# Polysketch attention and hash routing on one core: the first heads taken one by one, and routing steps reordered

## The chip, the core and the metric

The kernel runs on one core of a Trainium2 chip. The metric is the device time of one launch in microseconds (us); lower is better. A core has five engines that run side by side, each with a queue of its own, in order: TensorE (PE) multiplies matrices, VectorE (DVE), ScalarE (ACT) and GpSimd (POOL) work element by element, and SyncE (SP) here only issues transfers. PE's weight loads stand in the profile as PEld. Transfers (DMA) are issued from SP and ACT, gathers and scatters by lists of rows from POOL.

## What is computed

Attention without a softmax: q and k are mapped to 64 features, the products of two sketches of 8 numbers each, and k's features are summed with v into one 64 x 32 matrix per head. Its output, as 4352 rows of 128, goes to a mixture of experts in which a token's number alone picks one of 8 experts.

```python
def phi(x):                                   # q, k, v: (4, 4, 1088, 32)
    a = np.einsum('rd,bhsd->bhsr', S1, x)     # S1, S2: (8, 32)
    b = np.einsum('rd,bhsd->bhsr', S2, x)
    return np.einsum('bhsi,bhsj->bhsij', a, b).reshape(*x.shape[:-1], r * r)
q_p, k_p = (phi(q), phi(k))
kv = np.einsum('bhsf,bhsd->bhfd', k_p, v)
z = np.sum(k_p, axis=2)
num = np.einsum('bhsf,bhfd->bhsd', q_p, kv)
den = np.einsum('bhsf,bhf->bhs', q_p, z)[..., None] + 1e-06
attn = num / den
x = attn.transpose(0, 2, 1, 3).reshape(4352, 128)
expert_idx = token_ids * np.int64(2654435761) % np.int64(8)
# for each expert e, rows of its tokens:
out[mask] = np.maximum(x[mask] @ w1[e], 0.0) @ w2[e]      # w1: (8, 128, 1024), w2: (8, 1024, 128)
```

## The kernel before

Every engine's order is written by hand: `tc.manual_schedule` (L92) keeps instructions on each engine in the order of the program's text. What sets the order around the change is therefore the order of calls, and each engine waits where an operand isn't there yet.

Attention goes over 4 batches, b = 0 to 3, each with 4 heads (H) of 1088 rows: 1024 in the main part, 8 rows (T) to each of 128 partitions, and 64 in a tail; the tails of all batches are worked together in batch 0. The steps of a batch, with the tiles' names:

- `load_main` (L114) loads k, q and v of a batch by SP; only k of batch 0 comes in two parts of two heads. `load_tail` loads the tails. Loads of later batches are held back by a one-element write on ACT (`A.memzero`) into the tile.
- `turned`, `turned_all` (L472, L483): PE transposes 4 rows of a head at once (T_ps), 8 transposes per tensor, in two banks of PSUM; ACT copies them to kT or qT. The pool of these banks (`bank`) has 4.
- `s_products` (L505): PE multiplies kT or qT by S (ab_ps); both sketches come out. S itself is given as 64-bit numbers: DVE turns them into 32 bits (s_rep), and PE and DVE spread them (`s_turned`, L282).
- `first_copied` (ACT) copies the first sketch, `features` (DVE, L527) multiplies it by the second: kp for k, f for q, two instructions each.
- `values` (POOL, a part by ACT in batch 0) copies v into va, with a column of ones beside it; `kv_products` (PE, L554) sums kp times va into kv, `kv_diagonal` (ACT) copies kv to m.
- `q_turned` (L581): PE transposes f (fT_ps), ACT and DVE copy it to fT by the list EVICT = (A, V, A, V); `x_products` multiply fT by m into xe.
- `denominators` (DVE), `x_main` and `x_tail` (POOL) divide: xs; `x_rows` (SP) stores them to a table in DRAM, x_rows.

Routing is spread between these steps, mostly on DVE: `route_scan` numbers the tokens of each expert, `route_counts` sums over partitions on PE, `route_places` and `route_order` rank the experts by load, `route_bases` and `route_ranks` give every token a digit, `route_parts` and `route_slots` (with a chain on POOL) its slot, `route_in_tile`, `route_rows` and `route_tiles` make one-hot matrices, and `route_list` multiplies them on PE into the list of rows (get, put). The name pos is used for the place of a token and, after its last use in `route_slots`, for another value, which the loop for overflow at the end reads.

Then come the experts: 16 groups of about 256 to 320 tokens. POOL gathers their rows by the list from x_rows (`fetch_tile`), PE transposes the first groups' rows (`bring`; later groups are transposed by DMA), `layer1` and `layer2` multiply, and POOL scatters the results. The gathers of the first group (of batches 0 and 1 alone) wait for the stores of both batches. `beside` (L1006) lists what stands between the products: `at(g, c, f)` puts f after step c of group g; `bring(1)` stands at step 6 of group 0, and layer1 of group 1 follows step 7.

Before all this PE runs six products of no use (`keep_busy(WARM)`, L219), on tiles of ones.

Of the kernel before, what the change touches and what calls it, by code (L numbers as in the profile page):

```python
# [30 lines left out]
def kernel(  # L31
# [64 lines left out]
    for i, (s, eng) in enumerate(((S1, nc.sync), (S2, nc.scalar))):  # L96
        eng.dma_start(s64[i * R:(i + 1) * R], _words(s).rearrange("r (d two) -> r d two", two=2))
# [16 lines left out]
    def load_main(src, b, tag, ahead=None):  # L114
        t = load.tile([P, H, T, D], F32, tag=tag, name=f"{tag}{b}")
        if ahead:
            ahead(t[:, 0, 0, 0:1])
        rows = src[b, :, 0:SM, :].rearrange("h (p t) d -> p h t d", t=T)
        parts = 2 if (b, tag) == (0, "k") else 1
        for i in range(parts):  # L120
            hs = slice(i * H // parts, (i + 1) * H // parts)
            nc.sync.dma_start(t[:, hs], rows[:, hs])
        return t
# [46 lines left out]
    k_tail = load_tail(k, "k_tail")  # L170
    k_t.append(load_main(k, 1, "k"))
    q_t.append(load_main(q, 1, "q"))
    q_tail = load_tail(q, "q_tail")
    v_tail = load_tail(v, "v_tail")
    k_t.append(load_main(k, 2, "k"))
# [43 lines left out]
    def keep_busy(n):  # L219

        if n == 0:
            return
        p = ps_o.tile([P, 512], F32, tag="o", name="idle")
        for _ in range(n):
            nc.tensor.matmul(p[:], warm[:].to_broadcast([P, P]), warm[:].to_broadcast([P, 512]), start=True, stop=True)
# [153 lines left out]
    late, slot, gap, over = (const.tile([P, C], F32, name=n) for n in ("late", "slot", "gap", "over"))  # L379
# [9 lines left out]
    def route_slots():  # L389

        V_ = nc.vector
        V_.tensor_scalar(late[:], pos[:], 0.0, 1.0, op0=OP.max, op1=OP.min)
# [7 lines left out]
        V_.scalar_tensor_tensor(pos[:], place_t[:], float(GD), pos[:], op0=OP.mult, op1=OP.add)  # L400

        G_ = nc.gpsimd
        G_.tensor_scalar(over[:], pos[:], float(GL), 0.0, op0=OP.subtract, op1=OP.max)
# [146 lines left out]
    def values(b, ts=slice(0, T), copy=nc.gpsimd.tensor_copy):  # L550

        copy(vas[b % 2][:, ts, :, 0:D], v_t[b][:, :, ts].rearrange("p h t d -> p t h d"))  # L552

    def kv_products(b, kp, ts, kv=None):  # L554

        kv = kv or x_bank([P, H // 2, DA], "kv")
        for t in ts:
            (f, v_) = (kp[:, t], vas[b % 2][:, t]) if t < T else (f_tail[:, 0, b % TT], va_tails[b // TT][:, b % TT])
            for pr in range(H // 2):
                for h in range(2):  # L560
                    nc.tensor.matmul(kv[h * R * R:(h + 1) * R * R, pr], f[:, 2 * pr + h].rearrange("p i j -> p (i j)"),  # L561
                                     v_[:, 2 * pr + h], start=(t == 0 and pr == 0), stop=(t == T), skip_group_check=True,
                                     tile_position=(0, h * R * R))
        return kv
# [157 lines left out]

    def turn_in(k):
# [12 lines left out]

    A, V = nc.scalar, nc.vector
    EVICT = (A, V, A, V)
    s_turned(x_bank)
    kT, half = turned(k_t[0], "kT")  # L740
    for pr in range(H // 2):
        for g in range(GQ):
            hs = slice(2 * pr, 2 * pr + 2)
            nc.scalar.copy(kT[:, g, hs], half(g, range(H)[hs])[:])
    route_experts()
    route_scan()
    nc.scalar.copy(cp[:], seq[:, :, C - 1])
# [6 lines left out]
    values(0, slice(0, T // 2))  # L754
    qT = turned_all(q_t[0], "qT")
    cnt = route_counts()
    route_places(cnt)
    route_order()
    abq, aq, f = ab_bank(), first_of_ab(), feature_tile("f")
    s_products(abq, qT, range(GQ))  # L760
    first_copied(aq, abq, range(GQ))
    values(0, slice(T // 2, T), nc.scalar.copy)
    kv = kv_products(0, kp, range(T))
    features(f, aq, abq, range(GQ))
    kT = turned_all(k_t[1], "kT")
    route_bases(cnt)
    digits = route_ranks()
    route_order_end()
# [10 lines left out]
    for b in range(B - 1):  # L779
        last = b == B - 2  # L780
        if b > 0:
# [5 lines left out]
        fT = q_turned(f, (A, A, A, A) if last else EVICT)  # L787
        if b == 0:
            tail_ps = bank([P, 2, TT, P], "tail_ps")
# [5 lines left out]
            for u, va_tail in enumerate(va_tails):  # L795
                rows = tail_rows(u * TT)
                nc.gpsimd.tensor_copy(va_tail[rows, :, :, 0:D], v_tail[rows])
            route_parts(digits)
            tail_features(tail_products(tailT))
# [21 lines left out]
        if b == 0:  # L821
            q_t.append(load_main(q, 2, "q", A.memzero))
            kv_products(0, None, range(T, T + 1), kv)
            m = kv_diagonal(0, kv)
            tail_f_turned()
        values(b + 1)
        if b == 1:
            v_t.append(load_main(v, 3, "v", A.memzero))
            for g in range(GQ):
                x_rows(0, g)  # L830
            x_tail_rows(0)
            route_rows(0)
            route_tiles()
            route_rows(1)
# [7 lines left out]
        if last:  # L842
            load_expert(0, (2,), A.memzero)
            features(kp, ak, abk, range(GQ))
# [4 lines left out]
        if not last:  # L849
            for g in range(GQ):  # L850
                x_main(b, g, nc.gpsimd)
            x_tail(b, nc.gpsimd)
# [169 lines left out]
    at(0, 6, bring, 1, o_bank)  # L1022
# [96 lines left out]
    with tc.If(turns > 0):  # L1119
        with tc.For_i(0, turns):  # L1120
# [20 lines left out]
            nc.vector.tensor_scalar(at[:], pos[:], of[:, 1:2], float(GL), op0=OP.subtract, op1=OP.subtract)  # L1141
# [69 lines left out]
```

## Time and profile before

| | us |
|---|---|
| median of 3 runs | 178.16 |
| lowest, highest | 177.83, 178.74 |
| the profiled execution | 180.07 |
| its span, first to last instruction | 178.1 |
| PE busy in the span | 171.0 |
| DVE busy | 98.0 |
| POOL busy | 94.6 |
| ACT busy | 66.9 |

A profile shows one execution, whose own time is 180.07 us; the span is what lies between its first and last instruction. Durations come from it, so a sum of them is to be compared with 180.07, not with the median. Times in the text count from the span's start. A timeline row has start, duration, engine, line, operation, the tiles out<-in with their shapes, the number of instructions merged, and in brackets the idle time before it with what ended it. A line can be that of a helper that several steps share. The list of waits has, for each pair, the total, the count and the longest; these are its largest rows that are not in the experts' part:

```profile
POOL va L552 <- DMA v<-in_v_dram: 6.5, 2, 3.8
POOL over L403 <- DVE pos L400: 5.0, 1, 5.0
ACT m L570 <- PE kv L561: 4.8, 3, 2.3
ACT first_of_ab L525 <- PE ab_ps L510: 3.7, 6, 0.7
```

### The profile page before, as it was taken

What the parts mean: (1) busy time and instruction counts of PE and PEld (TensorE: products, weight loads), DVE (VectorE), ACT (ScalarE), POOL (GpSimd) and SP (SyncE); (2) the same over time, 40 slices, a digit from 0 to 9 for tenths busy, and PEclk for the clock granted to TensorE, in tenths of its full rate; (3) what the DMA queues carried; (4) which work ended last, traced back from release to release, by engine and by line L of the source; (5) the groups of instructions that cost most, each with busy time, mean ns of one, the idle gap of its engine ahead of it and who ended that gap; (6) DMA issues with size and microseconds to landing.
All of it is one profiled execution on the core that took longest, in us unless ns stands there. A gap on an engine that the chain in (4) does not pass through costs nothing. (4 is left out here: it accounts for less than half of the span.)

```text
span 178.1 us, 4338 instructions
## 1 busy us (share of the span) xinstructions
PE 171.0 (96%) x1569; PEld 144.5 (81%) x1569; DVE 98.0 (55%) x312; ACT 66.9 (38%) x179; POOL 94.6 (53%) x134
## 2 busy tenths in 40 slices
PE   6999999999999999999999999999999999999990
PEld 1899899999987888888777777788888777778990
DVE  5589999996945425365444343634457552442330
ACT  3456685874643242232341323233141332321330
POOL 7324239364176657177776612775655760406752
PEclk9999999999999999999999999999999999999999
DMA  4998057565495969994992663386342522210111
GB/s 131 296 250 241 13 145 250 139 254 172 141 292 166 317 170 189 168 309 103 234 166 75 186 170 74 103 213 142 78 96 53 117 65 54 56 36 29 43 36 32
DMA packets 39302, 25.83 MB, mean 145 GB/s; under 512 B 20884, under 2 KB 35477, under 8 KB 39280
## 3 DMA queue, kind: packets, MB, share of 16 engines
q1 hardware_dynamic: 36880, 20.98, 46.9%
q0 software_dynamic: 2240, 4.53, 9.0%
q8 instruction: 13, 0.21, 0.5%
q14 instruction: 9, 0.07, 0.1%
q10 hardware_dynamic: 160, 0.04, 0.1%
HBM read 17.41 MB, written 4.52 MB: 123 GB/s over the span
## 5 line engine op out<-in xcount | busy, mean ns | idle before, releaser
L897 PE MATMUL op<-hT,w 128*128 128x256 f32 (+8 forms) x256 | 76.3, 389 | 0.0
L650 DVE TENSOR_SCALAR hT<-hp 128x256 f32<-128x256 f32 (+9 forms) x68 | 29.1, 427 | 57.2 <-PE hp L889 54.7
L897 PEld LDWEIGHTS op<-hT,w 128*128 128x128 f32 x256 | 47.5, 190 | 10.5
L900 POOL DMA_INDIRECT out_dram<-os,put x35 | 35.3, 1008 | 28.3 <-DVE os L958 11.8
L648 ACT ACTIVATE hT<-hp 128x256 f32<-128x256 f32 (+9 forms) x68 | 26.6, 391 | 63.0 <-PE hp L889 62.9
L642 POOL DMA_INDIRECT xg<-x_rows,idx x33 | 34.0, 1030 | 28.4 <-DVE idx L709 17.4
L889 PE MATMUL hp<-xT_late,w 128*128 128x320 f32 (+8 forms) x144 | 41.7, 385 | 0.0
L889 PE MATMUL hp<-xT,w 128*128 128x256 f32 x128 | 37.6, 382 | 0.1
L889 PEld LDWEIGHTS hp<-xT_late,w 128*128 128x128 f32 x144 | 25.3, 190 | 4.7
L889 PEld LDWEIGHTS hp<-xT,w 128*128 128x128 f32 x128 | 23.9, 190 | 5.9 <-ACT hT L648 0.5
L532 DVE TENSOR_TENSOR f<-first_of_ab,ab_ps 128x1024 f32<-128x1024 f32 x8 | 9.4, 1212 | 1.8 <-ACT first_of_ab L525 1.8
L958 DVE COPY os<-turned 128x256 uint16<-128x256 uint16 (+1 forms) x26 | 7.7, 336 | 4.1 <-DMA turned<-half 3.9
L532 DVE TENSOR_TENSOR kp<-first_of_ab,ab_ps 128x1024 f32<-128x1024 f32 x8 | 9.3, 1200 | 1.2 <-ACT first_of_ab L525 1.2
L561 PE MATMUL kv<-va,kp 128*64 128x33 f32 x256 | 8.6, 224 | 0.1
L552 POOL COPY va<-v 128x1024 f32<-128x1024 f32 (+1 forms) x4 | 3.7, 932 | 9.2 <-DMA v<-in_v_dram 6.5
L561 PEld LDWEIGHTS kv<-va,kp 128*64 128x64 f32 x256 | 8.0, 138 | 0.8 <-ACT va L552 0.2
L597 PE MATMUL x_ps<-m,fT 128*64 128x66 f32 x256 | 8.3, 222 | 0.0
L597 PEld LDWEIGHTS x_ps<-m,fT 128*64 128x64 f32 x256 | 7.8, 137 | 0.5 <-issue 0.3
L937 ACT COPY half<-op 128x256 uint16<-128x256 uint16 x16 | 5.2, 375 | 7.5 <-PE op L897 7.5
L578 PE MATMUL fT_ps<-ident,f 128*128 128x128 f32 x64 | 7.7, 273 | 0.0
L623 POOL TENSOR_TENSOR xs<-xe,den 128x512 f32<-128x512 f32 x6 | 6.7, 1142 | 1.4 <-ACT qT L486 1.4
L728 DVE COPY xh<-xg 128x256 uint16<-128x256 uint16 (+1 forms) x26 | 6.9, 307 | 0.5 <-DMA xg<-x_rows,idx 0.5
(190 smaller groups left out, 170.5 us busy)
## 6 DMA issues: line engine op xcount, KB each, us to landing
w<-in_moe_w_dram SPq DMA_DIRECT2D x22, 256.0 KB, 4.5
w<-in_moe_w_dram SPq DMA_DIRECT2D x5, 512.0 KB, 4.6
q<-in_q_dram SPq DMA_DIRECT2D x4, 512.0 KB, 4.5
v<-in_v_dram SPq DMA_DIRECT2D x4, 512.0 KB
x_rows<-xs SPq DMA_DIRECT2D x8, 256.0 KB
k<-in_k_dram SPq DMA_DIRECT2D x3, 512.0 KB
out_dram<-os,put POOLq DMA_INDIRECT x35, 2.6
xg<-x_rows,idx POOLq DMA_INDIRECT x33, 3.4
```

Source lines behind the costliest of these rows:

```text
L532: nc.vector.tensor_tensor(dst[:].rearrange("p t h i j -> p (t h) i j")[:, r], a[:, r].unsqueeze(3).to_broadcast(shape), rows_of_ab(ab)[:, ...
L561: nc.tensor.matmul(kv[h * R * R:(h + 1) * R * R, pr], f[:, 2 * pr + h].rearrange("p i j -> p (i j)"), v_[:, 2 * pr + h], start=(t == 0 and ...
L578: nc.tensor.transpose(p[:, t, pr], f[:, 2 * i + t, 2 * pr:2 * pr + 2].rearrange("p h i j -> p (h i j)"), ident[:])
L597: nc.tensor.matmul(p[r, t, 2 * pr:2 * pr + 2].rearrange("p h d -> p (h d)"), fT[:, lo + t, pr, r], m[:, pr].rearrange("p h d -> p (h d)"), ...
L642: nc.gpsimd.indirect_dma_start(out=dst, out_offset=None, in_=x_dram[0:rows], in_offset=bass.IndirectOffsetOnAxis(ap=idx, axis=0), bounds_c ...
L648: nc.scalar.activation(dst, src, AF.Relu if relu else AF.Copy)
L650: return nc.vector.tensor_scalar(dst, src, 0.0, None, op0=OP.max).ins
L728: nc.vector.tensor_copy(xh[:, x * w:(x + 1) * w], _half(xg3[k][:].rearrange("p a b -> p (a b)")[:, 0:w], x))
L889: nc.tensor.matmul(hp[:, 0:hi - lo], w1[:, g % E, c * P:(c + 1) * P], x_columns(first_of(g) + lo, first_of(g) + hi), start=True, stop=True)
L897: nc.tensor.matmul(ops[g][:, 0:hi - lo], w2[:, g % E, c], hTs[g][:, c, lo:hi], start=(c == 0), stop=(c == FC - 1))
L900: st_ = nc.gpsimd.indirect_dma_start(out=out[:], out_offset=bass.IndirectOffsetOnAxis(ap=idx, axis=0), in_=src, in_offset=None, bounds_che ...
L958: nc.vector.tensor_copy(_half(os[:].rearrange("p a b -> p (a b)"), x)[:, 0:n * DM], tts[x][:, 0:n].rearrange("p a b -> p (a b)"))
```

## The change

- Loads: both parts of S are issued from ACT. k and q of batch 0 come in four parts, a head each, v of batch 0 in two. In SP's order k and q of batch 1 go ahead of the tails, k of batch 2 ahead of v's tail.
- First batch: `turned_head` transposes one head of k or q (two transposes, one bank, one copy of 256 columns on ACT). For k, S is spread after the third head. For q, each head's products with S follow the next head's transposes; their bank comes from another pool (`x_bank`). Behind the products of k stand two products of no use (`keep_busy(2, bank)`).
- `values` of batch 0 is split by heads instead of rows, the first half on ACT, the second on POOL; kv goes first over the first pair of heads, then over the second. `route_scan` follows the features of k on DVE, and `route_counts` follows kv on PE; features of q come ahead of `route_places`.
- Batch 0: `route_bases` and `route_ranks` go behind the copies of fT, `tail_features` ahead of `route_parts`, `route_order_end` last. k of batch 2 is transposed in batch 0, half ahead of the tail's kv and half behind fTt_ps. ACT makes all copies of fT in batch 1.
- xs of batch 0: its denominators, divisions and stores go to batch 1, behind the one-hot matrices.
- `route_slots` writes a tile of its own, behind, first, where the last step wrote pos; POOL's chain and the loop for overflow read it.
- `bring(1)` becomes two steps of one tile each, at steps 5 and 6, both copied by DVE.

```diff
--- before
+++ after
@@ -93,8 +93,8 @@
     s64 = const.tile([2 * R, D, 2], I32)
-    for i, (s, eng) in enumerate(((S1, nc.sync), (S2, nc.scalar))):
-        eng.dma_start(s64[i * R:(i + 1) * R], _words(s).rearrange("r (d two) -> r d two", two=2))
+    for i, s in enumerate((S1, S2)):
+        nc.scalar.dma_start(s64[i * R:(i + 1) * R], _words(s).rearrange("r (d two) -> r d two", two=2))
     tok = const.tile([P, C, 2], I32)
@@ -116,7 +116,7 @@
         rows = src[b, :, 0:SM, :].rearrange("h (p t) d -> p h t d", t=T)
-        parts = 2 if (b, tag) == (0, "k") else 1
+        parts = {(0, "k"): H, (0, "q"): H, (0, "v"): H // 2}.get((b, tag), 1)
         for i in range(parts):
@@ -167,12 +167,12 @@
     v_t.append(load_main(v, 0, "v"))
-    k_tail = load_tail(k, "k_tail")
     k_t.append(load_main(k, 1, "k"))
     q_t.append(load_main(q, 1, "q"))
+    k_tail = load_tail(k, "k_tail")
     q_tail = load_tail(q, "q_tail")
+    k_t.append(load_main(k, 2, "k"))
     v_tail = load_tail(v, "v_tail")
-    k_t.append(load_main(k, 2, "k"))
     v_t.append(load_main(v, 1, "v"))
@@ -216,11 +216,11 @@
-    def keep_busy(n):
+    def keep_busy(n, psum=None):
...
...
             return
-        p = ps_o.tile([P, 512], F32, tag="o", name="idle")
+        p = psum([P, 512], "idle") if psum else ps_o.tile([P, 512], F32, tag="o", name="idle")
         for _ in range(n):
@@ -376,7 +376,7 @@
-    late, slot, gap, over = (const.tile([P, C], F32, name=n) for n in ("late", "slot", "gap", "over"))
+    late, slot, gap, over, behind = (const.tile([P, C], F32, name=n) for n in ("late", "slot", "gap", "over", "behind"))
...
@@ -389,6 +389,7 @@
         V_ = nc.vector
+        V_.scalar_tensor_tensor(behind[:], place_t[:], float(GD), pos[:], op0=OP.mult, op1=OP.add)
         V_.tensor_scalar(late[:], pos[:], 0.0, 1.0, op0=OP.max, op1=OP.min)
@@ -397,10 +398,9 @@
         V_.scalar_tensor_tensor(slot[:], place_t[:], float(GE), slot[:], op0=OP.mult, op1=OP.add)
-        V_.scalar_tensor_tensor(pos[:], place_t[:], float(GD), pos[:], op0=OP.mult, op1=OP.add)
...
         G_ = nc.gpsimd
-        G_.tensor_scalar(over[:], pos[:], float(GL), 0.0, op0=OP.subtract, op1=OP.max)
+        G_.tensor_scalar(over[:], behind[:], float(GL), 0.0, op0=OP.subtract, op1=OP.max)
         G_.tensor_scalar(over[:], over[:], float(2 * ST * P), None, op0=OP.mult)
@@ -547,16 +547,16 @@
-    def values(b, ts=slice(0, T), copy=nc.gpsimd.tensor_copy):
-
-        copy(vas[b % 2][:, ts, :, 0:D], v_t[b][:, :, ts].rearrange("p h t d -> p t h d"))
-
-    def kv_products(b, kp, ts, kv=None):
+    def values(b, hs=slice(0, H), copy=nc.gpsimd.tensor_copy):
+
+        copy(vas[b % 2][:, :, hs, 0:D], v_t[b][:, hs].rearrange("p h t d -> p t h d"))
+
+    def kv_products(b, kp, ts, kv=None, pairs=range(H // 2)):
...
...
             (f, v_) = (kp[:, t], vas[b % 2][:, t]) if t < T else (f_tail[:, 0, b % TT], va_tails[b // TT][:, b % TT])
-            for pr in range(H // 2):
+            for pr in pairs:
                 for h in range(2):
@@ -720,6 +720,12 @@
+    def bring_tile(k, j):
+        i = tiles_of(k)[0] + j
+        xp = o_bank([P, P], "xp")
+        nc.tensor.transpose(xp[:], xg3[k][:, j], ident[:])
+        evict(1, x_columns(i * P, (i + 1) * P), xp[:])
+
     def turn_in(k):
@@ -734,38 +740,52 @@
+    def x_main_all(b):
+        for g in range(GQ):
+            x_main(b, g, nc.gpsimd)
+        x_tail(b, nc.gpsimd)
+
     A, V = nc.scalar, nc.vector
     EVICT = (A, V, A, V)
-    s_turned(x_bank)
-    kT, half = turned(k_t[0], "kT")
-    for pr in range(H // 2):
+    kT, _ = turned(k_t[0], "kT")
+
+    def turned_head(src, sT, h):
+        p = bank([P, GQ, P], "T_ps")
         for g in range(GQ):
-            hs = slice(2 * pr, 2 * pr + 2)
-            nc.scalar.copy(kT[:, g, hs], half(g, range(H)[hs])[:])
+            nc.tensor.transpose(p[:, g], src[:, h, g * Q:(g + 1) * Q].rearrange("p t d -> p (t d)"), ident[:])
+        nc.scalar.copy(sT[:, :, h], p[:])
+
+    for h in range(H):
+        turned_head(k_t[0], kT, h)
+        if h == 2:
+            s_turned(x_bank)
     route_experts()
-    route_scan()
-    nc.scalar.copy(cp[:], seq[:, :, C - 1])
     ak, kp = first_of_ab(), feature_tile("kp")
...
         features(kp, ak, abk[g], [g])
-    values(0, slice(0, T // 2))
-    qT = turned_all(q_t[0], "qT")
+    route_scan()
+    keep_busy(2, bank)
+    qT, _ = turned(q_t[0], "qT")
+    abq, aq, f = ab_bank(x_bank), first_of_ab(), feature_tile("f")
+    for h in range(H + 1):
+        if h < H:
+            turned_head(q_t[0], qT, h)
+        if h > 0:
+            s_products(abq, qT, range(GQ), [h - 1])
+    values(0, slice(0, H // 2), nc.scalar.copy)
+    first_copied(aq, abq, range(GQ))
+    values(0, slice(H // 2, H))
+    kv = kv_products(0, kp, range(T), pairs=(0,))
+    kv_products(0, kp, range(T), kv, (1,))
+    nc.scalar.copy(cp[:], seq[:, :, C - 1])
     cnt = route_counts()
+    features(f, aq, abq, range(GQ))
     route_places(cnt)
     route_order()
-    abq, aq, f = ab_bank(), first_of_ab(), feature_tile("f")
-    s_products(abq, qT, range(GQ))
-    first_copied(aq, abq, range(GQ))
-    values(0, slice(T // 2, T), nc.scalar.copy)
-    kv = kv_products(0, kp, range(T))
-    features(f, aq, abq, range(GQ))
     kT = turned_all(k_t[1], "kT")
-    route_bases(cnt)
-    digits = route_ranks()
-    route_order_end()
...
@@ -778,14 +798,16 @@
         last = b == B - 2
-        if b > 0:
+        if b > 1:
             kT = turned_all(k_t[b + 1], "kT")
...
             qT = turned_all(q_t[b + 1], "qT")
-        fT = q_turned(f, (A, A, A, A) if last else EVICT)
+        fT = q_turned(f, (A, A, A, A) if b > 0 else EVICT)
         if b == 0:
+            route_bases(cnt)
+            digits = route_ranks()
             tail_ps = bank([P, 2, TT, P], "tail_ps")
@@ -795,8 +817,9 @@
                 nc.gpsimd.tensor_copy(va_tail[rows, :, :, 0:D], v_tail[rows])
+            tail_features(tail_products(tailT))
             route_parts(digits)
-            tail_features(tail_products(tailT))
+            route_order_end()
         elif not last:
@@ -820,18 +843,23 @@
             q_t.append(load_main(q, 2, "q", A.memzero))
+            kT, half = turned(k_t[2], "kT")
+            nc.scalar.copy(kT[:, 0], half(0)[:])
             kv_products(0, None, range(T, T + 1), kv)
...
             tail_f_turned()
+            nc.scalar.copy(kT[:, 1], half(1)[:])
         values(b + 1)
...
             v_t.append(load_main(v, 3, "v", A.memzero))
+            route_rows(0)
+            route_tiles()
+            route_rows(1)
+            denominators(0)
+            x_main_all(0)
             for g in range(GQ):
...
             x_tail_rows(0)
-            route_rows(0)
-            route_tiles()
-            route_rows(1)
         features(f, aq, abq, range(GQ))
@@ -841,15 +869,16 @@
             load_expert(0, (2,), A.memzero)
+        if b == 0:
+            features(kp, ak, abk, range(GQ))
+        elif last:
             features(kp, ak, abk, range(GQ))
...
             features(kp, ak, abk, range(GQ))
-        if not last:
-            for g in range(GQ):
-                x_main(b, g, nc.gpsimd)
-            x_tail(b, nc.gpsimd)
+        if 0 < b and not last:
+            x_main_all(b)
         if b == 1:
@@ -1019,7 +1048,8 @@
         at(0, 3 + c, fetch_tile, 3, c)
-    at(0, 6, bring, 1, o_bank)
+    for j in range(tiles_of(1)[1]):
+        at(0, 5 + j, bring_tile, 1, j)
     at(1, 5, bring, 2)
@@ -1138,7 +1168,7 @@
             at = moe.tile([P, C], F32, tag="at", name="at", bufs=1)
-            nc.vector.tensor_scalar(at[:], pos[:], of[:, 1:2], float(GL), op0=OP.subtract, op1=OP.subtract)
+            nc.vector.tensor_scalar(at[:], behind[:], of[:, 1:2], float(GL), op0=OP.subtract, op1=OP.subtract)
             nc.vector.tensor_mul(at[:], at[:], own[:])
...
             rows = moe.tile([P, C, P], BF16, tag="hT", name="rows", bufs=2)
...
```

## The prediction

> **What bounds the kernel now.** I read the page first: TensorE (PE) is busy 171.0 us of 178.1, the next engine, VectorE (DVE), 98.0 us. Its slices say where PE is not full:
>
> ```profile
> span 178.1 us, 4338 instructions
> PE   6999999999999999999999999999999999999990
> DVE  5589999996945425365444343634457552442330
> ```
>
> Only the first slice (4.45 us each) and the end are thin. But busy is not full rate: the page says that ends of matmuls are modelled. So I took the timeline of PE and compared equal groups early and late:
>
> ```profile
> 0.98 2.74 PE L225 MATMUL idle<-warm 128*128 128x512 bf16 x6 [0.98 <-POOL warm L180]
> 4.75 0.26 PE L284 MATMUL s_ps<-ident,s_rep 16*128 16x16 f32 x1 [1.03 <-POOL is_early L211]
> 4.93 1.97 PE L477 MATMUL T_ps<-ident,k 128*128 128x128 f32 x8
> 6.83 1.98 PE L510 MATMUL ab_ps<-s_k,kT 128*64 128x64 f32 x32
> 8.74 1.80 PE L477 MATMUL T_ps<-ident,q 128*128 128x128 f32 x8
> ...
> 11.73 2.29 PE L561 MATMUL kv<-va,kp 128*64 128x33 f32 x64
> 13.95 1.09 PE L477 MATMUL T_ps<-ident,k 128*128 128x128 f32 x8
> 14.88 1.91 PE L578 MATMUL fT_ps<-ident,f 128*128 128x128 f32 x16
> ```
>
> Eight transposes take 1.97 us at 4.93 and 1.09 at 13.95; 32 products with S take 1.98 at 6.83 and (later rows) 1.10. PE runs at about half rate until some 10.2 us and then at the full one to the end. From 13.95 on groups follow one another with hardly a hole: between 58 and 170 us, the stretch table gives PE 112.00 of 112.00. So the end is set by when PE reaches L477 for k1 (13.95), plus the few holes after it. These I looked for as irregular gaps: T_ps of q1 takes 1.36 us at 17.06 instead of 1.06 to 1.09, because its bank waits for DVE's copy of fT (L585), which stands behind routing steps; kv of the tail waits at 21.05 for f_tail, ready at 20.91; around `bring(1)` some 0.4 us are lost:
>
> ```profile
> 17.04 1.27 DVE L585 COPY fT<-fT_ps 128x512 f32<-128x512 f32 x2
> 19.70 1.21 DVE L543 TENSOR_TENSOR f_tail<-first_of_ab,abt_ps 128x1024 f32<-128x1024 f32 x1
> ```
>
> Last, POOL, for what may hold PE at 48.07, the first gathered rows:
>
> ```profile
> 28.18 2.61 POOL L623 TENSOR_TENSOR xs<-xe,den 128x512 f32<-128x512 f32 x2
> 30.75 1.44 POOL L629 TENSOR_TENSOR xs_tail<-xe,den 64x128 f32<-64x128 f32 x1
> 34.90 1.05 POOL L552 COPY va<-v 128x1024 f32<-128x1024 f32 x1 [2.70 <-PE T_ps L477]
> 37.35 2.06 POOL L623 TENSOR_TENSOR xs<-xe,den 128x512 f32<-128x512 f32 x2 [1.41 <-ACT qT L486]
> 39.36 0.42 POOL L629 TENSOR_TENSOR xs_tail<-xe,den 64x128 f32<-64x128 f32 x1
> 39.73 1.03 POOL L552 COPY va<-v 128x1024 f32<-128x1024 f32 x1
> 42.77 1.29 POOL L642 DMA_INDIRECT xg<-x_rows,get  x1 [2.01 <-issue]
> ```
>
> The wait at 34.90 is named after PE, but v2's transfer, issued at 28.77, ends at about the same time, and that is what the copy needs.
>
> **What the Trainium skill says.** "TensorE: Matmul & The Clock Gate", section "What's actually happening": PE starts at half clock and gets the full one after a busy window of about 3.4 us; windows run free of the kernel. The trace agrees with half and full (421 against 273 ns for one transpose). Work from 0.98 to 3.7, then a hole of 1.03 us, was not enough here; the step came at about 10.2. The same page, "PE-mode transpose", says that transposes don't count as busy for this; the window that ended at 10.2 held half of them, so this trace speaks against that, or not clearly. [...]k's half (256 KB) lands 3.3 us after issue. "SBUF — State Buffer", "Who interferes with whom": DVE and GpSimd lock a shared port pair against each other. The trace agrees: xs at 28.18 beside DVE's route_rows takes 1.3 us each and at 37.35 1.03; DVE's row takes 2.13 us beside it and 1.28 alone.
>
> **The change, part by part**, against the profiled execution (180.07 us: span 178.1 and 1.97 around it; the median of the plain runs, 178.16, is 1.91 lower).
>
> Loads. k0 comes in four transfers from 0.82 (S no longer ahead on SP). Issue takes some 0.46 us each, so they go out at 0.82, 1.28, 1.75, 2.2; 128 KB should land some 2.9 us after issue (3.3 less the 0.4 that half the bytes need at 350 GB/s): 3.8, 4.2, 4.7, 5.1, the last as before. S2 goes behind S1 on ACT, 0.58 later; DVE's chain, 2.65 to 4.60, becomes about 3.1 to 5.0. q0 in four and v0 in two add four issues (1.9 us) on SP; q0's last part goes out at 4.2 and lands by 7.1 to 7.8, v0 by 9.9 as now (POOL starts on it at 9.96). In both instruction lists each of SP's transfers waits for the one eight before it, so the four added ones also bring waits: q0's later parts on S1, S2 and the first head of k0 (landed by 3.8), v0 on heads 1 and 2, k1 on head 3; all of these are in before SP gets there. k1 and q1 pass the tails, whose small rows now come last; the same bytes have to land before PE's 15.6 (they are in at 14.6 now), so I cost this at nothing. k2, which PE wants at about 19.5 instead of 24.25, is issued at 12.5 now and is ahead of v_tail then; nothing. If it came late, up to 1 us would show there.
>
> Head of PE. Transposes start at 3.85, not 4.93, half-rate pairs of 0.43 behind each landing; s_ps at 5.2, the last head done at 5.9, its copy (0.37) at 6.5, products from 6.0. The holes are now a few tenths each, so a busy window of 3.4 us can close at 4.4 to 7.6; I take 6.5. Products: 0.5 us at half rate and 22 of 32 at 26 ns: end 7.3. Two unused products at full rate 0.43: 7.75 (at half rate 0.85, as six took 2.74). Their bank is that of k's first head, long copied. They cost this, but q's first parts are there and ACT's first copy has its time. q: per head two transposes (0.22), copy 0.37, eight products (0.21); ACT's four copies with PE's returns make the chain: 7.75 to about 10.6. ACT then copies half of va (0.62, to 10.8) and kv starts at 10.9 instead of 11.73, without the hole at 12.6: 1.87 us, cnt 0.15 (it was earlier), so T_ps of k1 at 12.9: **1.05 us earlier.**
>
> Holes in batch 0. fT's copies come ahead of route_bases, T_ps of k2 (0.46) goes between ab and the tail's kv, tail_features ahead of route_parts: 0.25 and 0.25 us gone, **-0.5**. What is late next is DVE, busy without a hole from 12.35 to 40.9 now: from f at 11.2 (2.3), places 1.1, fT to 16.3 (0.5 waiting for PE), bases 2.3, f_tail 1.2, parts and order 1.5, f 2.3, slots 1.6, kp 2.3 it reaches 27.5, so kv of batch 1 can't keep its lead: **+0.3**. After it DVE gains: two fT copies (1.27) go to ACT, which has room (24 of 40 us), and row builds run without xs on POOL (2.13 becomes 1.28). `behind` replaces one step by one, and lets POOL start on `over` some 1.5 us earlier, but POOL then waits for slot as now: nothing. ACT's memzero ahead of q3's load is moved before fT's copies, so q3 leaves SP earlier; v2's stays behind them.
>
> bring_tile. The eviction of tile 1 (0.42 for both, before layer1 of chunk 1 waits 0.3 us for it at 55.98) gets a layer1 between, and only half a tile's eviction is left: **-0.3**. Its first tile must be there 0.86 us (one c) earlier; it was issued 1.56 us before the second, so it is.
>
> xs of batch 0 goes behind v2's copy on POOL. From v2's landing: va 1.05 and 0.15, xs 2.06, tail 0.42, xs 2.06, tail 0.42: 6.2 us, where now it is 5.0 (34.75 to 39.78). v2 is issued on ACT behind four fT copies; with k3 and q3 loaded earlier I expect the landing at 32 to 33.6 instead of 34.75, so rows of batch 1 stored between 1.6 us earlier and the same. PE comes to its first xp 1.2 us earlier, with 0.4 slack now; it stalls 0 to 0.9: **+0.3**. On SP the stores of batch 0 move from 33.3 to about 36 and meet those of batch 1 instead of v3's load; 0.2 of that is in the range.
>
> Sum: -1.05 - 0.5 + 0.3 - 0.3 + 0.3 = -1.25; 180.07 becomes 178.8 with a profile, 176.9 without.
>
> **Rivals.** (1) Everything passes: v2 lands early and DVE keeps up: -1.85 and a bit, 176.2. For: DVE waits 1.77 us at 42.6 now; against: the 6.2 us chain. (2) PE stays at half rate to 10 us as now (the free window falls badly, or arrival gaps spoil it): ab ends 7.8, unused products 0.85, q by heads at half rate to 11.7: the head gains nothing, the rest -0.2: 177.9. Some of the runs of before may also have stepped up earlier than the profiled one, which pulls the same way. (3) Slower: the first gather. If v2 lands at 34.75 as now, va, xs (with the 1.6 us that its first piece took beside DVE), tails and the second xs end at 40.9 to 42.5 instead of 39.78, the first xp moves by as much from 47.7, and PE, which can do nothing else there, is at 48.8 to 50.4 instead of 48.07; less 0.3: +0.4 to +2, I say 179.2. It decides from the point where v2 lands after about 34.0.
>
> **How the numbers follow.** 0.5% is 0.89 us, about what a measurement tells from no change: faster is below 177.27, slower above 179.05. Forecast 0.42 (176.2 to 177.7), everything passes 0.17, half rate 0.14, gather 0.27. Faster: 0.31 of the forecast's, 0.17, 0.02: 0.50. Slower: 0.16 of the gather's (what exceeds 179.05) and 0.02 of the half rate's: 0.18. The rest, 0.32, is the same. Range 175.9 to 179.6: the gather's upper part, about 0.1, and the low end of the first rival are left out.
>
> **What would show it.** T_ps of k in pairs from 3.9; ab_ps of k with medians below 314 ns; T_ps of k1 near 12.9; no long T_ps of q1 near 16; PE's first xp at 46.8 to 47.7 and who waits there; POOL's xs back to back behind va. It is wrong if T_ps of k1 isn't before 13.4, or if PE stands at the first xp for more than 1 us.

## The result and the profile after

| | before | after |
|---|---|---|
| median, timed together | 178.56 us (22 runs) | 179.34 us (22 runs) |
| lowest, highest | 177.83, 181.85 | 178.29, 180.53 |
| profiled execution, span | 180.07, 178.1 | 180.15, 178.1 |

The ratio is 1.0045, with an interval of 1.0023 to 1.0066. A faster kernel was forecast (176.9 us); this one is slower by 0.8 us in its median. Two later series of the same two kernels gave 1.0008 (0.9984 to 1.0031) and 1.0036 (1.0010 to 1.0062); the mean of the three is 1.0030, about 0.5 us. A fourth series, on a chip where every kernel took about 190 us, tells nothing (below). (Ratios leave disturbed executions out, medians don't.)

The head of PE came out as drawn up. The timeline of PE after:

```profile
3.51 1.56 PE L755 MATMUL T_ps<-ident,k 128*128 128x128 f32 x6
...
5.92 1.16 PE L510 MATMUL ab_ps<-s_k,kT 128*64 128x64 f32 x32
7.01 0.61 PE L225 MATMUL idle<-warm 128*128 128x512 bf16 x2
...
10.90 2.06 PE L561 MATMUL kv<-va,kp 128*64 128x33 f32 x64
...
12.98 1.07 PE L477 MATMUL T_ps<-ident,k 128*128 128x128 f32 x8
...
16.07 1.04 PE L477 MATMUL T_ps<-ident,q 128*128 128x128 f32 x8
```

32 products take 1.16 us and not 1.98, T_ps of k1 begins at 12.98, 0.97 us earlier than in the profile before, and the long T_ps of q1 is gone. PE's first gathered rows (xp) follow at 46.81 instead of 48.07 without a wait, and layer1's fourth group at 68.97 instead of 70.60. With a lead of 1.63 us at 69 us, both spans are 178.1 all the same. The stretches of PE show where the lead goes (columns: stretch, its length, busy time of PE and of the others, PE's clock, DMA share, GB/s):

```profile
58.00:72.00 14.00, 14.00 (x68) 12.30 (x67) 4.80 (x25) 4.56 (x13) 7.48 (x8) 1.00 1.00 193
72.00:77.00 5.00, 3.44 (x16) 2.73 (x15) 2.88 (x14) 0.77 (x2) 1.40 (x2) 1.00 0.86 231
77.00:170.00 93.00, 93.00 (x414) 75.14 (x413) 41.90 (x163) 26.39 (x75) 52.57 (x52) 1.00 0.47 110
```

PE stands for 1.56 us in one place. Its timeline (L918 is layer1, L926 layer2) and, next, that of DVE there (L650 evicts layer1, that is, copies its results out of PSUM; L987 is in `join_out`):

```profile
72.86 0.59 PE L926 MATMUL op<-hT,w 128*128 128x256 f32 x2
75.02 0.70 PE L918 MATMUL hp<-xT,w 128*128 128x256 f32 x2 [1.56 <-DVE idx L709]
```

```profile
68.23 0.94 DVE L650 TENSOR_SCALAR hT<-hp 128x256 f32<-128x256 f32 x2
...
73.86 0.31 DVE L987 COPY os<-turned 128x256 uint16<-128x256 uint16 x1 [4.67 <-DMA turned<-half]
74.34 0.31 DVE L987 COPY os<-turned 128x256 uint16<-128x256 uint16 x1 [0.17 <-DMA turned<-half]
74.55 0.42 DVE L650 TENSOR_SCALAR hT<-hp 128x256 f32<-128x256 f32 x1
```

The releaser named for PE (idx) ran in passing. What held it is `join_out`: DVE waits 4.67 us for the results of the first group, turned (transposed) by a DMA, and behind that in its queue stands the eviction of layer1's step c = 1 of the fourth group (74.55). layer1 has four banks, so c = 5 can't start before it. In the profile before the same wait was there, in DVE and then in PE:

```profile
73.67 0.31 DVE L958 COPY os<-turned 128x256 uint16<-128x256 uint16 x1 [2.86 <-DMA turned<-half]
74.25 0.32 DVE L958 COPY os<-turned 128x256 uint16<-128x256 uint16 x1 [0.27 <-DMA turned<-half]
74.47 0.42 DVE L650 TENSOR_SCALAR hT<-hp 128x256 f32<-128x256 f32 x1
```

```profile
74.94 0.70 PE L889 MATMUL hp<-xT,w 128*128 128x256 f32 x2
```

PE's c = 5 began at 74.94, right behind that eviction, which ended at 74.89. The wait cost next to nothing there, but in that execution it was a wall: a PE that came earlier would have run into it.

### The profile page after: what moved, and what is told of

The parts are those of the page before. It is cut to its first block, busy times and chain, and to the rows that moved or that the text cites. A ratio compares the mean times of both kernels' runs of the same rounds, so it can differ in the third digit from the quotient of the medians.

```text
span 178.1 us, 4354 instructions
## 1 busy us (share of the span) xinstructions
PE 170.3 (96%) x1571; PEld 143.0 (80%) x1571; DVE 96.2 (54%) x311; ACT 67.9 (38%) x183; POOL 93.0 (52%) x134
## 5 line engine op out<-in xcount | busy, mean ns | idle before, releaser
L926 PE MATMUL op<-hT,w 128*128 128x256 f32 (+8 forms) x256 | 76.3, 389 | 0.0
L650 DVE TENSOR_SCALAR hT<-hp 128x256 f32<-128x256 f32 (+9 forms) x68 | 29.1, 428 | 56.2 <-PE hp L918 53.4
L926 PEld LDWEIGHTS op<-hT,w 128*128 128x128 f32 x256 | 47.5, 190 | 10.5
L918 PE MATMUL hp<-xT_late,w 128*128 128x320 f32 (+8 forms) x144 | 41.7, 385 | 0.0
L918 PE MATMUL hp<-xT,w 128*128 128x256 f32 x128 | 37.7, 382 | 1.6 <-DVE idx L709 1.6
L918 PEld LDWEIGHTS hp<-xT,w 128*128 128x128 f32 x128 | 23.8, 190 | 7.5 <-DVE idx L709 2.0
L918 PEld LDWEIGHTS hp<-xT_late,w 128*128 128x128 f32 x144 | 25.3, 190 | 4.7
L987 DVE COPY os<-turned 128x256 uint16<-128x256 uint16 (+1 forms) x26 | 7.4, 329 | 5.3 <-DMA turned<-half 5.3
L578 PEld LDWEIGHTS fT_ps<-ident,f 128*128 128x128 f32 x64 | 7.0, 140 | 0.3
```

The costliest lines, as they stand in the source:

```text
L578: nc.tensor.transpose(p[:, t, pr], f[:, 2 * i + t, 2 * pr:2 * pr + 2].rearrange("p h i j -> p (h i j)"), ident[:])
L650: return nc.vector.tensor_scalar(dst, src, 0.0, None, op0=OP.max).ins
L918: nc.tensor.matmul(hp[:, 0:hi - lo], w1[:, g % E, c * P:(c + 1) * P], x_columns(first_of(g) + lo, first_of(g) + hi), start=True, stop=True)
L926: nc.tensor.matmul(ops[g][:, 0:hi - lo], w2[:, g % E, c], hTs[g][:, c, lo:hi], start=(c == 0), stop=(c == FC - 1))
L987: nc.vector.tensor_copy(_half(os[:].rearrange("p a b -> p (a b)"), x)[:, 0:n * DM], tts[x][:, 0:n].rearrange("p a b -> p (a b)"))
```

## Experiments

Ratios are to the kernel before, timed in the same series. PE's way splits into four stretches, read in each profile: to T_ps of k1, from there to layer1's first product, to the first product of layer1's second group, and to PE's end (some 4.6 us of scatters follow it). The recorded expectations call the third of these points "the third group"; by the program it is the second, since a group has eight steps and each step stands in the profile as two products. "Full clock from" is read from durations: a transpose takes 421 ns before it and 273 after.

| profile | full clock from | T_ps k1 | to layer1 | to 2nd group | to PE's end | PE's end |
|---|---|---|---|---|---|---|
| before | 10.23 | 13.95 | 35.78 | 6.77 | 117.02 | 173.51 |
| before_4 | 8.79 | 13.05 | 35.27 | 6.73 | 116.89 | 171.95 |
| before_join_late | 8.04 | 12.81 | 35.33 | 7.17 | 116.89 | 172.20 |
| bring_join | 8.87 | 13.35 | 35.67 | 6.40 | 116.89 | 172.31 |
| bring_join_2 | 9.91 | 14.05 | 35.27 | 6.47 | 116.89 | 172.68 |
| head_only | 4.48 | 12.99 | 36.92 | 7.10 | 116.89 | 173.90 |
| after | 5.25 | 12.98 | 35.48 | 6.40 | 118.72 | 173.59 |
| after_4 | 6.87 | 13.46 | 35.33 | 6.39 | 117.48 | 172.66 |
| after_5 | 5.60 | 13.09 | 35.34 | 6.65 | 116.89 | 171.97 |
| after_whole_bring | 5.56 | 13.08 | 35.34 | 7.44 | 116.89 | 172.75 |
| join_late | 5.11 | 12.94 | 35.33 | 6.39 | 116.89 | 171.56 |
| join_late_2 | 5.60 | 12.99 | 36.34 | 6.39 | 117.67 | 173.39 |
| jl_tails | 5.73 | 13.19 | 35.68 | 6.66 | 116.89 | 172.42 |
| jl_xs0 | 9.99 | 14.60 | 36.67 | 6.54 | 116.89 | 174.71 |
| jl_warm7 | 4.28 | 12.99 | 35.34 | 6.40 | 116.98 | 171.70 |
| fetch_early | 3.77 | 12.98 | 39.17 | 7.70 | 116.89 | 176.74 |

The first five have before's head, the others the changed one. The profile of fetch_early is of an execution of 183.32 us, where the quickest took 178.88: its long stretches are not those of a usual execution.

**The join moved** (four steps later, in both kernels, three runs).

```diff
-        c = FC if g < E else 5
+        c = FC + 4 if g == 2 else FC if g < E else 5
```

> The changed kernel with one call moved: the first join_out of VectorE goes from (group 3, c 0) to (group 3, c 4), and its three scatters from c 1 to 3 to c 5 to 7. Theory (wall): in the changed kernel PE is 1.65 us ahead at 60 us and loses it between 72.9 and 75.0, because VectorE waits from 69.2 to 74.3 for the transposed results of the first group, with the eviction of layer1's c 1 behind it in its queue, and PE has four banks only. With the join behind it, no idle time of PE between 60 and 100 us, layer1 of late columns begins near 83.0 instead of 84.6, time 177.5 to 178.1 where the changed kernel has 179.3. Rival (transfers): all transfers of 60 to 76 us are too slow for a PE that is earlier; then PE stands at the next thing that they bring (rows of group 4 or weights, 75 to 80 us), and the time is 178.9 to 179.4.

> The kernel before with the same call moved. Theory (wall): in its profile layer1's c 5 of group 3 begins at 74.94, with a bank that came free at 74.89, so the wall is there without holding PE: 178.6, within 0.3 of before. If the runs without a profile stand nearer to the wall than the profiled one (their PE gets its full clock earlier), it gains up to 0.8: 177.8. Rival (transfers): no change, 178.6.

> The changed kernel with the join moved, a second time. Theory (wall): 116.9 from layer1's third group to PE's end; ratio to before 0.997 to 1.001. Theory (head): no gain from the head, T_ps of k1 at 12.8 to 13.2, or near 14.6 where a window of the clock is missed. Rival: as for the changed kernel, 1.002 to 1.006.

join_late: no idle time of PE, late columns from 82.59, a profiled execution of 178.13 us, 2 us less than the changed kernel's. But the median of 22 runs is 179.18, ratio 1.0008 (0.9985 to 1.0032), and the second series gave 1.0032 (1.0001 to 1.0062), where the changed kernel itself stood at 1.0008 beside it. The profile is as the wall theory has it, the median is not: a gain of 0.3 to 0.6% from moving the join was expected, and none is there. So the wall is in single profiles, and it is not shown that it sets the usual time. before_join_late: 1.0018 (0.9998 to 1.0038), no gain, and a surprise: its PE was as early as the changed kernel's (layer1 from 48.14, in after from 48.46). In join_late_2 a wait comes back at 76.5 us, at the join_in that now stands ahead of the moved join.

**The head alone; PE's program longer.** head_only is before with the changed loads and head, and later steps as before. fetch_early is the changed kernel with 24 narrow products of no use at the start instead of 6 wide ones (`keep_busy` takes the width as `cols`):

```diff
...
-    keep_busy(WARM)
+    keep_busy(4 * WARM, cols=128)
```

> The kernel before with the changed head alone (loads by heads, k and q by heads, two unused products, order of routing up to route_order); later steps, xs of batch 0 and bring(1) as before. Theory (wall): T_ps of k1 is at about 13.0 and PE about 1 us ahead of before at 60 us in the profile, and the lead is lost by 75.0: 178.4 to 179.4, not faster than before. Rival (the later parts cost it): the head alone is faster than before by 0.8 to 1.2: 177.4 to 177.8.

> The changed kernel with the six products of no use at the start as 24 of 128 columns instead of 6 of 512: the same columns, 18 more products and weight loads in PE's program, so each later fetch of PE's instructions (256 of them, 16 KB) comes some 3.9 us earlier in PE's work. Rival (fetch): the fetch at 71.6 holds the transposes that all 16 DMA engines do together until 73.35; with it near 67.7 the transposed results land near 72, VectorE's join is 1.5 us earlier, PE's wait at 73 is gone or under 0.3 us and the time falls to about 178. Theory (wall, with slow transfers as its cause and the fetch not): the join stays at 73.5 to 74 and the time at 179.3 within 0.4.

head_only is slower: 1.0074 (1.0038 to 1.0110, from 9 runs). In its profile the lead is lost long before 75 us. PE's timeline there:

```profile
15.64 0.38 PE L492 MATMUL tail_ps<-ident,k_tail 128*128 128x128 f32 x2
17.07 0.41 PE L492 MATMUL tail_ps<-ident,q_tail 128*128 128x128 f32 x2 [1.05 <-DMA q_tail<-in_q_dram]
```

So neither theory had its cause. Of the 16 parts of q_tail's second half 15 had landed by 15.24, the last at 16.94. fetch_early did not test the wait at 73 us: in its profile PE stood 3.3 us at the first gathered rows. Its ratio is 1.0036 (1.0004 to 1.0069), from 7 of 23 executions; the median of all is 183.36. PE's timeline:

```profile
48.27 0.33 PE L720 MATMUL xp<-ident,xg 128*128 128x128 f32 x1 [1.54 <-DMA xg<-x_rows,get]
50.36 0.33 PE L720 MATMUL xp<-ident,xg 128*128 128x128 f32 x1 [1.76 <-DMA xg<-x_rows,get]
```

The gather was issued at 43.78 (41.91 after), since of the stores of batch 1's rows 15 parts had landed by 41.14 and one came at 42.81. What a later or earlier fetch does to the join stays open.

**Parts undone on top of the moved join, and the kernel before with two edits.** jl_tails puts the loads of the tails back; jl_xs0 puts xs of batch 0 back in batch 0; jl_warm7 has `WARM = 7`; bring_join is before with bring_tile and the moved join.

```diff
+    k_tail = load_tail(k, "k_tail")
     k_t.append(load_main(k, 1, "k"))
     q_t.append(load_main(q, 1, "q"))
-    k_tail = load_tail(k, "k_tail")
     q_tail = load_tail(q, "q_tail")
+    v_tail = load_tail(v, "v_tail")
     k_t.append(load_main(k, 2, "k"))
-    v_tail = load_tail(v, "v_tail")
```

> The changed kernel with the join moved, and the loads of the tails back in their old places (k_tail ahead of k1, q_tail and v_tail ahead of k2). The run with the join moved had a profile of 178.13 us but a median of 179.18. Theory (tails): in other executions the second half of q_tail, which lands at 14.7 to 15.3 in the profiles of this load order and at 17.0 in that of the head alone, comes after PE's 15.86 and holds PE by up to 1 us; with the old order it lands by 14.7, and the median falls by 0.4 to 0.8, to 178.4 to 178.8. Rival (no tails): 179.2 within 0.3.

> The changed kernel with the join moved, and xs of batch 0 back in batch 0 on POOL (stores ahead of route_rows, denominators ahead of kp), as before. Theory (first gather): in many executions xs of both batches behind v2's copy makes the first gather late (43.8 in one profile, with 3.3 us of holes of PE behind it, 41.2 in another), so with xs of batch 0 early the median falls by 0.4 or more: under 178.8, and none over 181. Rival: v2's copy then waits for xs beside VectorE as before and VectorE's row builds are slower again; median the same within 0.3, or slower by up to 0.5.

> The changed kernel with the join moved and seven products of no use at the start instead of six: they end at 3.2 to 3.4, T_ps of k begins at 3.51, so the hole of PE from 2.9 to 3.5 is gone at no cost. Theory (clock): in some executions the hole, and the short ones between the heads' landings, spoil a window[...] of PE's clock, and the full clock comes at 9 to 10 instead of 3.8 to 6.8, which costs up to 1.7 us; the executions of 180.1 to 180.5 (4 of 22 with the join moved) go, the median falls by 0.2 to 0.5, to 178.7 to 179.0. Rival: the hole does no harm; 179.2 within 0.2 and the same spread.

> The kernel before with two edits: bring(1) as bring_tile by tiles, as in the changed kernel, and the join moved. Theory (the head gains nothing over a usual execution of before, since there T_ps of k1 begins at 12.8 and not at 13.95, and of the rest only bring_tile gains): layer1's first group to its third takes 6.4 us instead of 7.2, the median is 0.5 to 0.8 below before: 178.3 to 178.6 where before has 179.1. Rival (the head's gain is real): it stays at 179.1 within 0.3, and slower than with the whole change and the join moved by 0.5 or more.

> The kernel before with bring_tile and the join moved, a second time: 0.9985 with an interval that holds 1 in the first. Theory (the head gains nothing, bring_tile 0.4 to 0.8): ratio 0.995 to 0.999, the lowest of the three. Rival: 0.999 to 1.002.

jl_tails 1.0016 (0.9993 to 1.0039) and jl_warm7 1.0028 (1.0002 to 1.0054) are what join_late was: no gain from either that these runs can tell. jl_xs0 is slower, 1.0061 (1.0033 to 1.0089), by 0.6 to 0.8 us against the other two, so xs of batch 0 behind v2's copy is no loss and rather a gain; the first-gather theory falls. Its profile also shows the changed head with the full clock at 9.99:

```profile
6.05 1.98 PE L510 MATMUL ab_ps<-s_k,kT 128*64 128x64 f32 x32
7.96 1.03 PE L225 MATMUL idle<-warm 128*128 128x512 bf16 x2
...
12.52 2.06 PE L561 MATMUL kv<-va,kp 128*64 128x33 f32 x64
```

T_ps of k1 then begins at 14.60, later than in any profile of before. bring_join gave 0.9985 (0.9963 to 1.0007) and 1.0019 (0.9997 to 1.0042): 6.40 and 6.47 us to the second group as expected, but less gain than expected or none, and no version here beats before beyond its interval.

**The two kernels again.**

> The kernel before, unchanged, a second time. Theory (a late clock): the first profile of before (180.07) is a slow one of its executions, since PE got its full clock at 10.23; the three profiles with this head so far have T_ps of k1 at 13.95, 12.81 and 13.35. Here it is under 13.6, the profiled time under 179.6, and the interval of the ratio holds 1. Rival: 13.95 is the usual case; T_ps of k1 at 13.8 to 14.1 again.

> The changed kernel, unchanged, a second time. Theory (wall): PE stands again at layer1's c 5 of group 3 (72 to 75 us) for 0.8 to 2 us, behind VectorE's first join_out, and from the third group of layer1 to PE's end it takes 117.7 to 118.9 instead of 116.9; T_ps of k1 at 12.9 to 13.2, or at 14.0 to 14.7 if a window of the clock is missed; ratio to before 1.002 to 1.006. Rival (the first profile was a chance): no idle time of PE over 0.3 us there, 116.9, and the loss is ahead of 60 us.

> The kernel before once more, for its profile. Theory (a late clock): T_ps of k1 between 12.7 and 13.6, time under 179.6. Theory (wall): where PE is early (T_ps of k1 under 13.2) it stands at layer1's c 5 of group 3 too, for 0.3 to 1.3 us, and from layer1's third group to PE's end it takes 117.2 to 118.2 instead of 117.0. Rival: T_ps of k1 at 13.8 to 14.1 and 117.0.

> The changed kernel once more, for its profile. Theory (wall): as for the second: 117.7 to 118.9 from layer1's third group to PE's end, with PE idle behind the first join_out. Rival: 116.9 and no wait there, with a loss ahead of 60 us (T_ps of k1 after 14, or a wait at the first gather).

> The kernel before, for its profile. Theory (a late clock was the first profile's): T_ps of k1 between 12.1 and 13.4, as in the four profiles with this head since (12.17 to 13.35), and the profiled time 177.6 to 179.3. Rival: 13.8 to 14.1 and 180.

> The changed kernel, unchanged, beside the one with the join moved. Theory (wall): from layer1's third group to PE's end 117.5 to 118.9 us, with PE idle near 73 to 75; ratio to before 1.002 to 1.006, and 0.3 to 0.6% above the one with the join moved. Rival (the first profile was a chance): 116.9, no wait there, and the two kernels within 0.15% of one another.

The first four fell on a chip where every kernel took about 190 us, with waits of PE between 83 and 98 us that no other profile has; the ratios are 1.0038 (0.9981 to 1.0096) for before against itself and 0.9996 (0.9902 to 1.0090) for after, which tells nothing. after_2 has no wait at the join, after_3 one of 0.88 us. Their heads: T_ps of k1 at 13.19 and 12.17 before, 12.78 and 13.93 after. In both of before the transposes of k ran at the full clock from the first (273 ns), and still T_ps of k1 came only at 13.19 in one of them, since PE waited 1.81 us for q. before_4, near the median with its 178.66 us, shows what an ordinary execution of before can look like. Its timeline of PE:

```profile
4.46 1.97 PE L477 MATMUL T_ps<-ident,k 128*128 128x128 f32 x8 [0.16 <-DMA k<-in_k_dram]
6.35 1.98 PE L510 MATMUL ab_ps<-s_k,kT 128*64 128x64 f32 x32
8.26 1.33 PE L477 MATMUL T_ps<-ident,q 128*128 128x128 f32 x8
```

```profile
13.05 1.09 PE L477 MATMUL T_ps<-ident,k 128*128 128x128 f32 x8
...
16.16 1.06 PE L477 MATMUL T_ps<-ident,q 128*128 128x128 f32 x8
```

Full clock from 8.79, kv from 10.83 (after: 10.90), T_ps of k1 at 13.05 and no long T_ps of q1: this execution of before has the head that I wanted from the change. Its DVE at the join:

```profile
70.16 0.31 DVE L958 COPY os<-turned 128x256 uint16<-128x256 uint16 x1 [0.78 <-DMA turned<-half]
70.82 0.31 DVE L958 COPY os<-turned 128x256 uint16<-128x256 uint16 x1 [0.35 <-DMA turned<-half]
```

The expectation that an early PE of before stands at the join is wrong: DVE's copies come 3.5 to 3.7 us earlier than in the first profile of after, and PE doesn't wait. after_4 has a wait (DVE's two copies at 71.70 and 73.42, 117.48 to the end).

**bring_tile undone in the changed kernel.**

```diff
-    for j in range(tiles_of(1)[1]):
-        at(0, 5 + j, bring_tile, 1, j)
+    at(0, 6, bring, 1, o_bank)
```

> The changed kernel with bring(1) whole at (0, 6) as before, the rest changed. Theory (given back at the join): layer1's first to third group 6.7 to 7.2 us instead of 6.4, from the third group to PE's end 116.9 to 117.3, where the changed kernel has 117.5 to 118.7; SP issues the first turned results 3.2 us or more ahead of group 3's first product (2.6 to 3.0 in the changed kernel); median within 0.3 of the changed kernel's. Rival (kept): 117.4 or more and a median 0.4 to 0.7 above the changed kernel's.

> The changed kernel beside it. Theory (given back): from layer1's third group to PE's end 117.3 to 118.8 with PE idle between 72 and 76; ratio to before 1.000 to 1.005. Rival: 116.9 and no wait.

The ratio is 1.0018 (1.0000 to 1.0036), and the changed kernel's beside it 1.0036: undoing bring_tile loses no time. In the profiles it takes 7.44 us to the second group instead of 6.65, but part of that is a late gather, at which the whole bring stood:

```profile
54.97 0.33 PE L720 MATMUL xp<-ident,xg 128*128 128x128 f32 x1 [0.47 <-DMA xg<-x_rows,idx]
```

after_5's profile has no wait of PE at the join, against both expectations. Its DVE:

```profile
69.89 0.31 DVE L987 COPY os<-turned 128x256 uint16<-128x256 uint16 x1 [0.49 <-DMA turned<-half]
71.87 0.32 DVE L987 COPY os<-turned 128x256 uint16<-128x256 uint16 x1 [1.67 <-DMA turned<-half]
```

The first copy comes 3.97 us earlier than in the first profile of after (73.86). A smaller part of that is the queue of SP. It issues the first turned results at 65.58 in after_5:

```profile
60.77 0.46 SPq L638 DMA_DIRECT2D x_rows<-xs_tail  x1
...
65.58 2.47 SPq L979 DMA_TRANSPOSE turned<-half  x2
```

and in the first profile of after at 66.33, since the store ahead of it waited for POOL's xs_tail (POOL idle 2.08 us at 61.02; the profile names ACT's copy of xT there, and a gather for the 1.44 us at 60.35 in after_5):

```profile
61.53 0.46 SPq L638 DMA_DIRECT2D x_rows<-xs_tail  x1
...
66.33 2.46 SPq L979 DMA_TRANSPOSE turned<-half  x2
```

That is 0.75 us. The other 3.2 are the transfer's own: from issue to DVE's first copy it took 7.5 us in after, 5.4 in after_4 and 4.3 in after_5, and 6.9 and 4.6 in before and before_4. Why it varies so is not shown. The transposes go out 2.64 us ahead of the fourth group's first product in after, 3.04 in after_4, 3.61 in after_5 (their last stretch is 1.8, 0.6 and 0 us longer than 116.89), 4.28 with bring whole, 3.81 and 3.56 in before and before_4. So bring_tile brings PE forward, but not this chain of xs_tail, store and transposes, and less is left for a slow transfer.

## Why the prediction was wrong

The step that failed is the base of the sum and what was built on it: two terms counted the lateness of one execution as time to be saved (the head is worth 0.2 us and not 1.05, the holes nothing and not 0.5), and the sum took it that a lead at 60 us reaches the end (the join gives back 1.8, 0.6 and 0 us of it).

**The base.** I took the 1.91 us between before's profiled execution and its median for a cost of the profile and carried the sum from one to the other ("180.07 becomes 178.8 with a profile, 176.9 without"). A profile costs no such thing: after_4 was profiled at 179.35 with a median of 179.34, join_late at 178.13 with one of 179.18, before_4 at 178.66 where the series had 178.99. The first profile of before was one late execution, and two terms of the sum measured its lateness.

**Head, -1.05: mis-sized.** T_ps of k1 at 12.9 was right (12.94 to 13.19 in nine of eleven profiles of the table, 13.46 and 14.60 in two). What it was compared with was not: before's head gives 12.81 to 14.05 in five profiles. The means are 13.21 and 13.44, a gain of 0.2 us, less than profiles of one and the same head differ among themselves. The changed head gets the full clock at 3.8 to 6.9 in ten of eleven profiles (before's at 8.0 to 10.2 in the five of the table), but spends it on its chain of ACT's copies, which I had put at 7.75 to 10.6 and which did end there. "TensorE: Matmul & The Clock Gate", section "What's actually happening", says that the window runs free of the kernel and that the transition varies from run to run; I had cited it, and my rival (2) had said that some runs of before may have stepped up earlier, but I gave the late one all the weight. The runs agree and go further: 8.04 to 10.23 for one and the same head, 2.2 us where the page gives 0.5 us to either side.

**Holes of batch 0, -0.5, and DVE gives back, +0.3.** before_4 has no such holes. From T_ps of k1 to layer1 before's order takes 35.27 to 35.78, after's 35.33 to 35.48 (36.34 in join_late_2, where a load was late): nothing, or 0.1 us.

**bring_tile, -0.3: about right.** Where PE doesn't wait for the second group's rows, the whole bring takes 6.77 and 6.73 us to the second group (before, before_4) and the tiles 6.39 to 6.47 in seven profiles (6.54 to 6.66 in three more): -0.3. Three profiles with the whole bring take 7.10 to 7.44, with PE idle for 0.35 to 0.47 us at a late gather; that is the gather's, not the step's.

**xs of batch 0, +0.3.** PE did not wait at the first rows in after, after_4 and after_5; the slower rival decides in none of them. By jl_xs0 the sign was wrong too.

**Loads.** The heads landed at 3.0, 3.5, 4.3 and 4.7, earlier than I said. That k1 and q1 pass the tails I had costed "at nothing", and that was wrong: q_tail is complete only at 14.7 to 15.8 in the three profiles of after, PE wants it from 15.9, and one late part cost 1.0 to 1.2 us in head_only and join_late_2, two of ten profiles with this order of loads (and in before_3, with the old order, on the chip of 190 us). jl_tails did not show that this sets the median.

**What was missing.** From a PE that is full "between 58 and 170 us" I concluded "So the end is set by when PE reaches L477 for k1", as if a lead at 60 us had to reach the end. The join gives back 1.8, 0.6 and 0 us in three profiles, a mean of 0.8, more than bring_tile brings. With -0.2, -0.1, -0.3 and +0.8 the four stretches come to +0.2 us, at the low end of the 0.1 to 0.8 us by which the three ratios put after above before. But moving the join did not take the loss away, and single profiles can't show how often a late transfer, at q_tail or at the join, comes. So it is shown that the head and the holes held no time to be saved in an ordinary execution; what makes the changed kernel slower in the median stays open.

## What to carry to other kernels

One profile is one execution: before a gain is counted from its late spots, see whether its time is near the median; if it isn't, its late spots are the first suspects, and they are no one's to save. An engine that is full from 58 us to the end may have other engines that arrive just in time: a wait of an engine off the path (here DVE's 2.86 us for a transfer) that ends as the path needs it can bound whatever arrives sooner. Bringing the busy engine forward also shortens the time that is left for the transfers that feed it, with their queue, if they don't come forward too.

## What the runs showed of the hardware

- A transfer ends with its last of 16 parts, and that one can be late alone: 15 parts of q_tail by 15.24 and the last at 16.94 (head_only), 14.92 and 16.70 (join_late_2), 41.14 and 42.81 (a store in fetch_early). Each time a fetch of PE's instructions, 16 KB in one packet, had begun before (13.75, 13.80 and 40.19, 1.0 to 1.5 us long). But every profile has such fetches, and in jl_xs0 one began at 13.82 without a part that late (the last at 15.49). That the fetch is the cause is not shown.
- The same two transposes of the first group took from 4.3 to 7.5 us from issue to the first copy of their result (after_5 and after). In the first profile of after many packets ended together while they were in flight: 18 that had started between 71.20 and 71.81 ended between 73.35 and 73.38, and before that 20 at about 70.4.
- In after_4 the full clock came at 6.87, after transposes at 3.51 to 5.01 and 5.42 to 6.04 and only 0.8 us of products with S. "TensorE: Matmul & The Clock Gate", "PE-mode transpose", has it that transposes don't count as busy; this trace is hard to read that way. In jl_xs0 much the same work (transposes at 3.51 to 5.05 and 5.43 to 6.12, products from 6.05) was not enough, and the full clock came at 9.99: the two traces together don't settle it. What the full clock does to a transpose is plain: 421 ns before it and 273 after.
